# Second-layer matmuls moved inside an iteration, and the later keys projected from rounded halves

## The chip, the cores and the metric

The kernel runs on one core of a Trainium2 chip. The metric is the device time of one execution in microseconds, given as the median of several runs. A profile of one further execution is read beside it. TensorE multiplies matrices into eight PSUM banks, VectorE, ScalarE and GpSimd work on elements, and SyncE's queue (SP) issues all transfers.

## The reference

Eight batch elements, eight heads, 576 positions, head width 64, 128 random features. First a linear attention:

```python
def phi(x):                                   # x is q or k, scaled by 64 ** -0.25
    h = np.einsum('bhsd,md->bhsm', x, omega) - sum(x * x) / 2
    return np.exp(h - np.max(h, axis=-1, keepdims=True)) / np.sqrt(m)
q_p, k_p = phi(q_s), phi(k_s)
kv, z = np.einsum('bhsm,bhsd->bhmd', k_p, v), np.sum(k_p, axis=2)
x = np.einsum('bhsm,bhmd->bhsd', q_p, kv) / (q_p . z + 1e-6)      # heads side by side: 4608 x 512
```

Then a feed-forward block on the 4608 rows of 512: `xn` is the layer norm of `x` times a gain, and the result is `x + relu(xn @ w_ch1) @ w_ch2`, with 2048 hidden values. All is fp32. The term `sum(x * x) / 2` is the same for all features of a row and falls out when the maximum is subtracted.

## The kernel before

**Tiles.** The 4608 rows are nine tiles of 512. For each tile TensorE does the first layer (f runs over 16 groups of 128 hidden values), and the second layer, which adds the products of all 16 groups up in four PSUM banks. Both layers work on rounded halves: each operand is a high part plus a low part in the rounded fp32 form, and a product is three matmuls (high by high, low by high, high by low). A run of such a matmul reads its moving operand in an order spread in runs of eight.

**From the third tile on** the first layer is done by `seven`, which computes a 2 by 2 block product with seven block products in place of eight. An iteration (tile t, g of 4, h of 2) has the products B11, T2, T1, T3, B21, B22 and N4, each six matmuls of 128 x 256 in `product` (L1124). They go to two banks, `one` (x and y) and `two` (v and z). VectorE and ScalarE put the results together in a buffer `u`: `second` (ScalarE copy L1194, VectorE addition L1187, done key `u2`), `fourth` (two additions, key `c22`), `third` (one addition of 512, key `cc`), and `first` and `third` write the rectified halves `hid` (L1211, L1213). Each iteration makes two groups of hidden values. Their second-layer work, `mm2` (L1270), is 24 matmuls of 128 x 256 for each group, and stands in the iteration after: once inside `seven`, where it yields from `between()`, and once behind it. In a tile's first iteration both are empty, as the two groups left over are done ahead of it. `hid` has two buffers, and a buffer is freed when its 24 matmuls are issued.

**Attention** is worked off beside this, about a tile ahead. Keys come in chunks of 128 positions (36 in all, 18 of them of the batch elements from the fifth on). `gen_k` projects a chunk: raw keys of two heads lie on partitions 0 to 63 and 64 to 127, and 8 full fp32 products of 64 rows (L653) fill two banks with 8 heads x 128 features. Then per bank a maximum (L565) and four exponentials (L583) into a `kp` buffer, of which there are two; odd chunks wait with their pair for the sums with the values (L620). Queries of the first four blocks are projected likewise (L700); the later ones by `gen_q2` from halves: raw queries lie twice, on partitions 0 to 63 and 64 to 127; ScalarE rounds all (L726), VectorE subtracts the rounded from the raw on the lower half (L728), and two matmuls of 512 columns with `om_hi` and `om_lo` follow (L1043). The maximum over the features of queries is GpSimd's (L759). The numerators (L833) give x, its statistics (L868) and `xn`, which is transposed (L969, L974) and, for the tiles of `seven`, combined (L990) and halved (L1016).

**Order.** All engines' instructions are issued in an order that a planner, `Plan`, makes when the kernel is built, from a cost for each step (`act`, `dve`, `us`) and a rank for each part. A part that yields `"get"` waits for a buffer, one that yields `wait` for a key. TensorE's feed-forward work has the last rank, so that attention matmuls are put into the stream as soon as they are planned to be ready. Results and buffers bound how far ahead attention gets: nine x tiles, three `kv` buffers, 14 `wide` buffers, and two PSUM banks (`b_at`) for all attention work. Weights of the second layer that leave room for this work are brought back by transfers (L429), and so are prepared sums of the first layer's weights (L502).

Of the kernel before, what the change touches and what calls it, by code (L numbers as in the profile page):

```python
# [14 lines left out]
F32R = mybir.dt.float32r  # L15
# [7 lines left out]
P = 128  # L23
B, H, S, D = 8, 8, 576, 64
M = 128
# [43 lines left out]
class Plan:  # L69
# [74 lines left out]
    def free(self, *names):  # L144
        for n in names:
            assert n not in self.places, n
            self.places[n] = self.cur.seen()
            self.cur.holds -= n[0] == "b" and 0 < self.cur.holds
            self.wake(lambda w: w[0] == "get" and n in w[1])

    def done(self, key):
        self.made[key] = self.cur.seen()
        self.wake(lambda w: w == ("wait", key))
# [41 lines left out]


@with_exitstack
def favor_ffn(ctx, tc, kT, kTr, vF, vR, qT, qD, omT, gT, w1, w2, out):

# [19 lines left out]
    def f32(ap):  # L221
        return ap.bitcast(F32)
# [13 lines left out]
    def dma(n):  # L236
        return "run", {SP: n * 4e-6 / 0.36}
# [13 lines left out]
    def wait(*key):  # L251
        return "wait", key
# [4 lines left out]
    def tile_of(tag, shape, dtype=F32, pool=None):  # L257
        pool = pool or (wp if tag[1].isdigit() and tag[0] == "w" else small if tag[0:2] in ("kv", "mb", "st") or tag[0] == "v" else sb)
        return pool.tile(shape, dtype, tag=tag, name=tag, bufs=1)
# [28 lines left out]
    eps = const.tile([P, 1], F32, name="eps")  # L288
    nc.gpsimd.memset(eps, EPS)

    nc.gpsimd.partition_all_reduce(tile_of("st5", [P, 64])[:, 0:1], eps, P, bass_isa.ReduceOp.max)

    def gen_ident():
        for blk in range(T // QB):
# [14 lines left out]
    if TILED:  # L309
        om = const.tile([P, M], F32, name="om")  # L310
        om_hi = const.tile([P, M], F32R, name="om_hi")
        om_lo = const.tile([P, M], F32R, name="om_lo")
    else:
        om = const.tile([P, 2, M], F32, name="om")
        nc.vector.memset(om, 0.0)
# [196 lines left out]
    def gen_keys():  # L512
        for b in range(B):
            if b == 1:
                yield wait("w", 2, GATE_K)
            if b % 2 == 0:
                t_kv = yield "get", n_kv
                kvs[b] = t_kv, heads_of(t_kv)

            for c in range(NFULL + (b % 2 == 0)):  # L520
                plan.cur.rank = NS * (b * S // T) + RK + 2 * c
                if c == NFULL:
                    t_kv = yield "get", n_kv
                    kvs[b + 1] = t_kv, heads_of(t_kv)
                first = n_first if b == 0 else ()
                k_turn = () if first else ((yield "get", turn["k"]),)
                t_k = yield "get", first + n_big
                kraw = tile_of(t_k, [P, NP, P])
                t_v = yield "get", first + n_v
                v = heads_of(t_v)  # L530
                plan.add(plan.cur.rank, gen_k(b, c, kraw, v, (t_k, *k_turn), t_v, n_kp + first))
# [5 lines left out]
    def kv_last(b):  # L537
        return kv_key(b, NFULL if b % 2 == 0 else NFULL - 1)

    pairs, held = {}, {}  # L540

    def gen_k(b, c, kraw, v, early, t_v, n_kp):
        rank = plan.cur.rank
        yield dma(2 * P * NP * P)
        nc.sync.dma_start(kraw, kT[b, c] if c < NFULL else kTr[b // 2])
        nc.sync.dma_start(v, vF[b, c] if c < NFULL else vR[b // 2])
        if c:
            yield wait("k", b, c - 1)
# [9 lines left out]
        def values():  # L558
            yield us(DVE, 0.08)
            nc.vector.memset(v[:, :, D : D + 1], 1.0)  # L560
            done(("v", b, c))
# [71 lines left out]
        def keep(n, s, t_b, pv):  # L633
# [8 lines left out]
            free(t_b)  # L642
            done((*kv_key(n, c), s))

        plan.add(rank, values())
        if TILED:
            t_b = yield "get", at_now(), 2
            yield us(PE, 1.15 if mlp_on else 1.0)
            pk = [bank(x).rearrange("p (a b) -> p a b", b=M) for x in t_b]
            for p in range(NP):  # L650
                for h in range(2):
                    a = slice(h * D, (h + 1) * D)
                    nc.tensor.matmul(pk[h][:, p], kraw[a, p], om[a], start=True, stop=True)  # L653
            for s in range(2):
                plan.add(rank, side(s, t_b[s], pk[s]))
        else:
            for s in range(2):
                t_b = yield "get", at_now()
                yield us(PE, 0.87)
                pk = bank(t_b).rearrange("p (a b) -> p a b", b=M)  # L660
                for p in range(2):
                    nc.tensor.matmul(
                        pk[:, 2 * p : 2 * p + 2], kraw[:, 2 * s + p], om, start=True, stop=True
                    )
                plan.add(rank, side(s, t_b, pk))
# [74 lines left out]
    def gen_om2():  # L740
        yield dve(M)
        nc.vector.tensor_copy(om_hi, om)
        yield dve(M)
        nc.vector.tensor_tensor(out=om_lo, in0=om, in1=f32(om_hi), op=ALU.subtract)
        done(("om2",))

    def features(blk, j, s, t_b, pq):
# [38 lines left out]
    def gen_block(blk, b_turn):  # L786
        rank = plan.cur.rank
        for j in range(2):
            if blk < WHOLE:
                plan.add(rank, gen_q(blk, j))  # L790
            else:
                for s in range(2):
                    plan.add(rank, gen_q2(blk, j, s))
        t_st = yield "get", n_st
        st = tile_of(t_st, [P, 64])
        for i in range(2):
            plan.add(rank + 6 + 2 * i, gen_x(2 * blk + i, t_st, st))
        for j in range(2):
            for s in range(2):
                yield wait("phi", blk, j, s)  # L800
        yield wait("num", 2 * blk)
        yield wait("num", 2 * blk + 1)
        plan.add(rank + 8, gen_over(blk, t_st))
        free(*(phis[blk, j, s][0] for j in range(2) for s in range(2)), b_turn)
# [324 lines left out]
    def seven(t, g, h, between):  # L1129


        cs = slice(h * P, (h + 1) * P)
        if not both:
            both.extend((yield "get", b_h, 2))
            both.extend(bank(x) for x in both[:2])
            (t_u,) = yield "get", n_w[2, SHARED[3]], 1
            both.append(tile_of(t_u, [P, 4, HC]))
        one, two, u = both[2:]
        x, y, v, z = one[:, 0:HC], one[:, HC:], two[:, 0:HC], two[:, HC:]

        def plain(row, col):
            def left(k, l):
                if row == col == 0:
                    return wparts[1, NK * g][:, k, l, cs]
                return wparts[1, NK * g + 2 * col + k][:, row, l, cs]
            return left

        def ring(i):
            def left(k, l):
                return rings[t, g, i][1][:, l, k, cs]  # L1150
            return left

        def run(out, i, left, name, start=False):
            if i:
                yield wait("ring", t, g, i)
                left = ring(i)
            for j in range(2):
                yield wait("x2", t, name, j)
            yield us(PE, 6 * 0.1134)
            product(out, left, ops[t, name][1], start)  # L1160
            if i and h == 1:
                free(rings[t, g, i][0])
            if g == NK - 1 and h == 1:
                free(ops[t, name][0])

        before = (t, g, h - 1) if h else (t, g - 1, 1) if g else (t - 1, NK - 1, 1)
        before = before if before[0] >= SEVEN else None
        yield wait("moved", g)
        yield "get", ("one",)
        yield from run(x, 0, plain(0, 0), "B11", True)  # L1170
        yield from run(y, 2, None, "T2")
        plan.add(MOST_URGENT, second(t, g, h, before, x, y, u))
        yield "get", ("two",)
        yield from run(v, 1, None, "T1", True)
        yield from run(z, 3, None, "T3")
        plan.add(MOST_URGENT, fourth(t, g, h, before, v, z, u))
        yield wait("u2", t, g, h)
        yield from run(x, 0, plain(0, 1), "B21")
        plan.add(MOST_URGENT, first(t, g, h, x, u))
        yield from between()  # L1180
        yield wait("c22", t, g, h)
        yield from run(v, 4, None, "B22")
        yield from run(z, 0, plain(1, 1), "N4")
        plan.add(MOST_URGENT, third(t, g, h, before, two, u))
# [14 lines left out]
    def fourth(t, g, h, before, v, z, u):  # L1199
        if before:  # L1200
            yield wait("hid", before[0], NK * before[1] + 2 + before[2])
        yield wait("u2", t, g, h)
        yield dve(HC)
        add(u[:, 3], v, u[:, 0])
        yield dve(HC)
        add(u[:, 3], z, u[:, 3])
        done(("c22", t, g, h))
# [167 lines left out]
SHARED, HOSTS = (4, 5, 6, 7, 2, 3, 0, 1), 8  # L1375
LENT = (*SHARED, *(f + HOSTS for f in SHARED))
LEAVE, RSIDE = 24, 24
WARM, COLD = 0.0, 5.0
RW, RS = -10, 1.0
RK, RQ = -36, -28  # L1380
# [52 lines left out]
```

## Time and profile before

| | |
|---|---|
| median of 3 runs | 968.72 us (968.61 to 970.42) |
| the profiled execution | 969.5 us, of which the span is 967.7 us |
| busy in the span | TensorE 956.8, VectorE 655.2, ScalarE 414.7, GpSimd 141.6 us |
| granted TensorE clock | 1.00 on average |
| instructions | 22723 |

The span is the time from the first to the last instruction of the program that the profiler recorded; the execution's own time also holds what lies around it. A matmul's end is modelled and lies behind the next one's start, so a busy share says that TensorE was never without a matmul, not how many it could have done; distances between starts say that.

### The profile page before, as it was taken

Reading aid. Unit: us, or ns where it says so; the run is one execution under the profiler, and the core shown is the slowest. Engines: PE = TensorE matmul, PEld = TensorE weight load, DVE = VectorE, ACT = ScalarE, POOL = GpSimd, SP = SyncE. Lnnn points to the kernel's source line nnn. Section 1 sums busy time; section 2 is a strip of 40 time slices with the busy share of each in tenths; the row PEclk is TensorE's granted clock in tenths of the full one; section 3 lists DMA queues with packets and bytes.
Section 4 is the critical chain, followed back from the end, with each engine's and each line's share of the span. In section 5 each row is a group of like instructions: output and inputs, shape, how many; then the busy total and the mean of one; then the engine's idle time right before and its main releaser. Section 6 shows DMA issues by size and latency. Waiting matters only on the chain.

```text
span 967.7 us, 22723 instructions
## 1 busy us (share of the span) xinstructions
PE 956.8 (99%) x9302; PEld 885.6 (92%) x9302; DVE 655.2 (68%) x1455; ACT 414.7 (43%) x989; POOL 141.6 (15%) x80
## 2 busy tenths in 40 slices
PE   9999999999999999999999999999999999999998
PEld 7778778887889999999999999999999999999998
DVE  5999999768988855794569547684688367345333
ACT  6488755443554634462336324461544132122111
POOL 3201434000323300140012200330023000000000
PEclk9999999999999999999999999999999999999999
DMA  9179742556646676856775567565765575568641
GB/s 338 39 257 408 249 153 79 178 178 203 215 154 218 208 229 216 256 178 199 231 251 175 178 206 268 201 215 193 235 222 183 177 249 162 190 212 268 214 145 44
DMA packets 73031, 197.77 MB, mean 204 GB/s; under 512 B 7776, under 2 KB 16096, under 8 KB 72928
## 3 DMA queue, kind: packets, MB, share of 16 engines
q1 hardware_dynamic: 72928, 196.33, 61.4%
q8 instruction: 73, 1.20, 0.5%
q14 instruction: 30, 0.25, 0.1%
HBM read 170.08 MB, written 26.21 MB: 203 GB/s over the span
## 4 chain that ended last, share of the span: by engine, by line
PE 83%; DVE 11%; DMA 3%; issue 1%; SPq 0%; ACT 0%; POOL 0%; DVEq 0%; ACTq 0%; POOLq 0%
PE b L1270 31%; PE b L1124 27%; PE b L1043 14%; PE b L833 3%; PE b L653 3%; PE b L620 3%; DMA w<-w 2%; DVE wide L762 1%; PE b L969 1%; DVE wide L383 1%; DVE mb L565 1%; DVE w L369 1%; DVE w L990 1%; DMA w<-vF 1%; DVE w L402 1%
## 5 line engine op out<-in xcount | busy, mean ns | idle before, releaser
L1270 PE MATMUL b<-w,hid 128*128 128x256 f32 x2688 | 333.5, 277 | 0.0
L1270 PEld LDWEIGHTS b<-w,hid 128*128 128x128 f32 x2688 | 318.2, 188 | 4.3
L759 POOL PARTITION_ALL_REDUCE wide<-wide x72 | 140.5, 1975 | 602.5 <-ACT wide L241 274.1
L1124 PE MATMUL b<-xnT,w 128*128 128x256 f32 x1344 | 177.3, 278 | 2.5 <-DVE w L1187 2.3
L1124 PEld LDWEIGHTS b<-xnT,w 128*128 128x128 f32 x1344 | 163.9, 188 | 6.2 <-DVE w L1187 4.3
L1187 DVE TENSOR_TENSOR w<-b,w 128x256 f32<-128x256 f32 x224 | 109.4, 488 | 54.6 <-PE b L1124 39.5
L1124 PE MATMUL b<-w,w 128*128 128x256 f32 x1008 | 127.3, 277 | 0.0
L1124 PEld LDWEIGHTS b<-w,w 128*128 128x128 f32 x1008 | 120.0, 188 | 1.4
L1213 DVE SCALAR_TENSOR_TENSOR hid<-w,hid 128x256 fp32r<-128x256 f32 x112 | 63.3, 565 | 80.4 <-ACT hid L1211 79.5
L1211 ACT ACTIVATE hid<-w 128x256 fp32r<-128x256 f32 x112 | 58.0, 524 | 135.2 <-DVE w L1187 69.9
L1043 PE MATMUL b<-w,hid 128*128 128x512 f32 x384 | 96.6, 392 | 0.0
L1043 PE MATMUL b<-xnT,w 128*128 128x512 f32 x360 | 91.5, 393 | 0.0
L583 ACT ACTIVATE kp<-b,mb 128x128 f32<-128x128 f32 x256 | 70.7, 385 | 42.3 <-DVE mb L565 42.1
L1211 ACT ACTIVATE hid<-b 128x256 fp32r<-128x256 f32 x56 | 21.6, 386 | 154.7 <-PE b L1270 140.5
L1043 PEld LDWEIGHTS b<-w,hid 128*128 128x128 f32 x384 | 70.5, 188 | 14.2 <-DVE hid L1107 0.2
L1213 DVE SCALAR_TENSOR_TENSOR hid<-b,hid 128x256 fp32r<-128x256 f32 x56 | 23.7, 423 | 84.8 <-ACT hid L1211 84.5
L1043 PEld LDWEIGHTS b<-xnT,w 128*128 128x128 f32 x360 | 66.1, 188 | 14.9 <-issue 1.3
L565 DVE TENSOR_REDUCE mb<-b 128x4 f32<-128x512 f32 x72 | 46.6, 682 | 20.6 <-PE b L653 20.6
L241 ACT COPY wide<-b 128x512 f32<-128x512 f32 x70 | 40.2, 592 | 42.3 <-PE b L1043 30.2
L767 ACT ACTIVATE wide<-wide 128x512 f32<-128x512 f32 x72 | 45.7, 638 | 28.9 <-DVE wide L762 26.5
L762 DVE TENSOR_TENSOR wide<-wide,wide 128x512 f32<-128x512 f32 x64 | 49.4, 775 | 7.4 <-POOL wide L759 7.3
L728 DVE TENSOR_TENSOR wide<-wide,wide 64x512 fp32r<-64x512 f32 x56 | 42.8, 771 | 8.8 <-ACT wide L726 7.2
(98 smaller groups left out, 982.4 us busy)
## 6 DMA issues: line engine op xcount, KB each, us to landing
w<-side SPq DMA_DIRECT2D x112, 512.0 KB, 6.4
w<-kept SPq DMA_DIRECT2D x112, 512.0 KB, 4.1
w<-w SPq DMA_DIRECT2D x32, 512.0 KB, 7.7
wide<-qD SPq DMA_DIRECT2D x56, 256.0 KB, 4.3
out<-x SPq DMA_DIRECT2D x36, 256.0 KB, 3.7
kept<-w SPq DMA_DIRECT2D x16, 512.0 KB, 3.3
side<-wide SPq DMA_DIRECT2D x32, 256.0 KB, 2.9
v<-vF SPq DMA_DIRECT2D x28, 260.0 KB, 5.1
```

Of the source, the lines that this page charges most:

```text
L565: nc.vector.tensor_reduce(out=mb[:, 4 * s : 4 * s + 4], in_=pk, axis=AX.X, op=ALU.max, negate=True)
L583: nc.scalar.activation(out=kp[:, j], in_=pk[:, i], func=AF.Exp, scale=1.0, bias=mb[:, j : j + 1])
L728: nc.vector.tensor_tensor(out=qs[D:P], in0=qraw[D:P], in1=f32(qs[D:P]), op=ALU.subtract)
L759: nc.gpsimd.partition_all_reduce(mx, qc, P, bass_isa.ReduceOp.max)
L762: nc.vector.tensor_tensor(out=qc, in0=pq if direct else qc, in1=mx, op=ALU.subtract)
L767: nc.scalar.activation(out=qc, in_=qc, func=AF.Exp)
L1043: nc.tensor.matmul(out.rearrange("p (c a b) -> p c a b", a=AW, b=BW), lhsT, rhs.rearrange("p (a c b) -> p c a b", a=AW, b=BW), start=start ...
L1124: nc.tensor.matmul(passes(out), left(k, l), passes(right[:, r, k]), start=start and k + l + r == 0, stop=k + r == 2, skip_group_check=True,)
L1187: nc.vector.tensor_tensor(out=out, in0=left, in1=right, op=ALU.add)
L1211: nc.scalar.activation(out=hl[:, 0, cols], in_=x, func=AF.Relu)
L1213: nc.vector.scalar_tensor_tensor(out=hl[:, 1, cols], in0=x, scalar=0.0, in1=f32(hl[:, 0, cols]), op0=ALU.max, op1=ALU.subtract)
L1270: nc.tensor.matmul(accs[i].rearrange("p (c a b) -> p c a b", a=AW, b=BW)[:, :, n * 8 : n * 8 + 8], hl[:, l, cs], w[:, r, n * HC : (n + 1) ...
```

## The change

The first edit moves one line in `seven`: `yield from between()`, the 24 second-layer matmuls, comes behind T3 and ahead of the wait for `u2`, where it was behind B21.

The second edit projects the keys of the batch elements 4 to 7 (`ROUND = 4`) as the later queries already are. The host lays these keys out twice, on partitions 0 to 63 and 64 to 127, in two transfers of four heads each (`kD`, `kDr`). `halved_keys` rounds them on ScalarE and subtracts on VectorE; `joined` multiplies each head's 128 x 128 stationary block by `om_both`, which holds omega's high and low part side by side, 256 columns, two heads to a bank; `summed` copies the low part's product out of PSUM and adds the high part's to it; maximum and exponentials then run from SBUF. `om_both` is made once in `gen_om2`. The raw loads are no longer issued with the values' load but behind the taking of a `kp` buffer. The statistics buffers `st` shrink from 64 to 32 columns.

```diff
@@ favor_ffn
+        om_both = const.tile([P, 2 * M], F32R, name="om_both")
@@ gen_keys
+                if b >= ROUND:
+                    t_v = yield "get", n_v
+                    plan.add(plan.cur.rank, gen_k(b, c, None, heads_of(t_v), k_turn, t_v, n_kp))
+                    continue
                 t_k = yield "get", first + n_big
@@ gen_k
-        yield dma(2 * P * NP * P)
-        nc.sync.dma_start(kraw, kT[b, c] if c < NFULL else kTr[b // 2])
+        yield dma((2 if kraw is not None else 1) * P * NP * P)
+        if kraw is not None:
+            nc.sync.dma_start(kraw, kT[b, c] if c < NFULL else kTr[b // 2])
         nc.sync.dma_start(v, vF[b, c] if c < NFULL else vR[b // 2])
...
+        def halved_keys(s):
+            t_k = yield "get", n_big
+            raw = tile_of(t_k, [P, 4 * P])
+            yield dma(4 * P * P)
+            nc.sync.dma_start(raw, kD[b - ROUND, c, s] if c < NFULL else kDr[b // 2 - ROUND // 2, s])
+            t_s = yield "get", n_big
+            ks = tile_of(t_s, [P, 4, P], F32R)
+            flat = ks.rearrange("p a b -> p (a b)")
+            yield act(4 * P)
+            nc.scalar.copy(out=flat, in_=raw)
+            yield dve2(4 * P)
+            nc.vector.tensor_tensor(out=flat[D:P], in0=raw[D:P], in1=f32(flat[D:P]), op=ALU.subtract)
+            free(t_k)
+            splits[b, c, s] = t_s, ks
+            done(("ks", b, c, s))
+
+        def joined(s):
+            yield wait("ks", b, c, s)
+            t_s, ks = splits.pop((b, c, s))
+            t_b = yield "get", at_now(), 2
+            plan.cur.after = max(plan.cur.after, plan.cur.end + LATE)
+            yield us(PE, 4 * 0.1134)
+            pk = [bank(x).rearrange("p (i l m) -> p i l m", i=2, l=2) for x in t_b]
+            for i in range(4):
+                nc.tensor.matmul(
+                    pk[i // 2][:, i % 2].rearrange("p l m -> p (l m)").rearrange("p (c a b) -> p c a b", a=8, b=8),
+                    ks[:, i], om_both.rearrange("p (a c b) -> p c a b", c=4, b=8), start=i % 2 == 0, stop=True,
+                    skip_group_check=True,
+                )
+            free(t_s)
+            o = kp[:, 4 * s : 4 * s + 4]
+            for h in range(2):
+                plan.add(rank, summed(s, h, t_b[h], pk[h]))
+            for h in range(2):
+                yield wait("kh", b, c, s, h)
+            yield dve2(4 * M)
+            nc.vector.tensor_reduce(out=mb[:, 4 * s : 4 * s + 4], in_=o, axis=AX.X, op=ALU.max, negate=True)
+            for j in range(4 * s, 4 * s + 4):
+                yield act(M, 1, 0.175)
+                nc.scalar.activation(out=kp[:, j], in_=kp[:, j], func=AF.Exp, scale=1.0, bias=mb[:, j : j + 1])
+            done(("kp", b, c, s))
+
+        def summed(s, h, t_b, pk):
+            o = kp[:, 4 * s + 2 * h : 4 * s + 2 * h + 2]
+            yield act(2 * M, 1, 0.13)
+            nc.scalar.copy(out=o, in_=pk[:, :, 1])
+            yield dve(2 * M)
+            nc.vector.tensor_tensor(out=o, in0=pk[:, :, 0], in1=o, op=ALU.add)
+            free(t_b)
+            done(("kh", b, c, s, h))
+
         plan.add(rank, values())
-        if TILED:
+        if kraw is None:
+            yield wait("om2")
+            plan.add(rank, halved_keys(0))
+            plan.add(rank, halved_keys(1))
+            plan.add(rank, joined(0))
+            yield from joined(1)
+        elif TILED:
@@ gen_om2
+        pieces = om_both.rearrange("p (a l c b) -> p l c a b", l=2, c=2, b=8)
+        nc.scalar.copy(out=pieces[:, 0], in_=f32(om_hi).rearrange("p (c a b) -> p c a b", c=2, b=8))
+        yield us(ACT, 0.25)
+        nc.scalar.copy(out=pieces[:, 1], in_=f32(om_lo).rearrange("p (c a b) -> p c a b", c=2, b=8))
@@ gen_block
-        st = tile_of(t_st, [P, 64])
+        st = tile_of(t_st, [P, 32])
@@ seven
         yield from run(z, 3, None, "T3")
         plan.add(MOST_URGENT, fourth(t, g, h, before, v, z, u))
+        yield from between()
         yield wait("u2", t, g, h)
         yield from run(x, 0, plain(0, 1), "B21")
         plan.add(MOST_URGENT, first(t, g, h, x, u))
-        yield from between()
         yield wait("c22", t, g, h)
```

## Rows read from the trace of the kernel before

**Rows 1.** The page: busy time of each engine, and the granted clock by slices.

```profile
PE 956.8 (99%) x9302; PEld 885.6 (92%) x9302; DVE 655.2 (68%) x1455; ACT 414.7 (43%) x989; POOL 141.6 (15%) x80
...
PEclk9999999999999999999999999999999999999999
```

**Rows 2.** The list of waits of TensorE's matmuls: us, times, longest us.

```profile
PE b L1124 <- DVE w L1187: 2.3, 4, 1.2
```

**Rows 3.** The instructions of L653, 317 to 697 us.

```profile
L653 PE MATMUL b<-om,wide x288: 272/272/373, 317.0 to 695.8; 64*128 64x128 f32 x144
```

**Rows 4.** Busy time of each engine in three stretches.

```profile
core 0: us, PE busy (x) PEld busy (x) DVE busy (x) ACT busy (x) POOL busy (x), PEclk, DMA share, GB/s
...
80.00:120.00 40.00, 40.00 (x318) 31.41 (x317) 39.91 (x70) 32.53 (x70) 13.73 (x6) 1.00 0.86 321
...
317.00:697.00 380.00, 379.54 (x4029) 367.19 (x4029) 244.22 (x564) 162.88 (x421) 52.75 (x28) 1.00 0.66 216
...
436.00:480.00 44.00, 44.00 (x426) 43.87 (x425) 20.87 (x47) 13.93 (x34) 1.05 (x1) 1.00 0.64 204
```

**Rows 5.** Timeline of TensorE around a key chunk and query halves: start, us, what.

```profile
420.52 2.20 PE L1270 MATMUL b<-w,hid 128*128 128x256 f32 x18
422.65 1.16 PE L653 MATMUL b<-om,wide 64*128 64x128 f32 x16
423.74 0.99 PE L1270 MATMUL b<-w,hid 128*128 128x256 f32 x6
424.57 2.21 PE L1124 MATMUL b<-w,w 128*128 128x256 f32 x18
...
432.56 0.39 PE L1043 MATMUL b<-wide,om_hi 128*128 128x512 f32 x1
432.79 0.40 PE L1043 MATMUL b<-wide,om_lo 128*128 128x512 f32 x1
433.02 1.52 PE L1124 MATMUL b<-xnT,w 128*128 128x256 f32 x12
```

**Rows 6.** Timeline of the ninth tile's second iteration (g 0, h 1).

```profile
885.89 2.20 PE L1124 MATMUL b<-w,w 128*128 128x256 f32 x18
...
887.27 1.21 DVE L1213 SCALAR_TENSOR_TENSOR hid<-w,hid 128x256 fp32r<-128x256 f32 x2 [0.48 <-ACT hid L1211]
...
889.66 2.88 PE L1270 MATMUL b<-w,hid 128*128 128x256 f32 x24
...
892.38 1.52 PE L1124 MATMUL b<-xnT,w 128*128 128x256 f32 x12
```

**Rows 7.** Groups of instructions by shape, 317 to 697 us: busy, mean ns, idle before.

```profile
L1187 DVE TENSOR_TENSOR w<-b,w 128x256 f32<-128x256 f32 x87 | 36.6, 420 | 14.8 <-PE b L1124 9.0 <-ACT w L1194 4.8
...
L728 DVE TENSOR_TENSOR wide<-wide,wide 64x512 fp32r<-64x512 f32 x28 | 19.5, 708 | 5.0 <-ACT wide L726 4.2
...
L726 ACT CAST wide<-wide 128x512 fp32r<-128x512 f32 x28 | 17.0, 617 | 7.8 <-DMA wide<-qD 7.8
...
L1194 ACT COPY w<-b 128x256 f32<-128x256 f32 x28 | 10.5, 374 | 19.0 <-PE b L1124 18.4
L990 DVE TENSOR_TENSOR w<-w 128x256 f32<-128x256 f32 x13 | 9.9, 761 | 0.3 <-ACT w L974 0.2
```

**Rows 8.** The page's transfers by line: KB each, us to landing.

```profile
wide<-qD SPq DMA_DIRECT2D x56, 256.0 KB, 4.3
```

**Rows 9.** Timeline at four places: idle us in brackets (PEld is the weight load).

```profile
332.10 0.39 PE L1043 MATMUL b<-wide,om_lo 128*128 128x512 f32 x1
332.63 0.97 PE L1124 MATMUL b<-xnT,w 128*128 128x256 f32 x6
...
492.65 1.64 PE L1124 MATMUL b<-xnT,w 128*128 128x256 f32 x12 [0.30 <-DVE w L1187]
...
738.30 0.76 PEld L1124 LDWEIGHTS b<-xnT,w 128*128 128x128 f32 x6 [1.37 <-DVE w L1187]
...
888.87 0.76 PEld L1124 LDWEIGHTS b<-xnT,w 128*128 128x128 f32 x6 [0.29 <-DVE w L1187]
```

More of the change, by code (lines that the diff above doesn't have):

```diff
@@ L197, in favor_ffn @@
 @with_exitstack
-def favor_ffn(ctx, tc, kT, kTr, vF, vR, qT, qD, omT, gT, w1, w2, out):
+def favor_ffn(ctx, tc, kT, kTr, kD, kDr, vF, vR, qT, qD, omT, gT, w1, w2, out):
     nc = tc.nc
@@ L289, in favor_ffn @@
     nc.gpsimd.memset(eps, EPS)
-    nc.gpsimd.partition_all_reduce(tile_of("st5", [P, 64])[:, 0:1], eps, P, bass_isa.ReduceOp.max)
+    nc.gpsimd.partition_all_reduce(tile_of("st5", [P, 32])[:, 0:1], eps, P, bass_isa.ReduceOp.max)
     def gen_ident():
@@ L538, in kv_last @@
         return kv_key(b, NFULL if b % 2 == 0 else NFULL - 1)
-    pairs, held = {}, {}
+    pairs, held, splits = {}, {}, {}
     def gen_k(b, c, kraw, v, early, t_v, n_kp):
         rank = plan.cur.rank
-        yield dma(2 * P * NP * P)
-        nc.sync.dma_start(kraw, kT[b, c] if c < NFULL else kTr[b // 2])
+        yield dma((2 if kraw is not None else 1) * P * NP * P)
+        if kraw is not None:
+            nc.sync.dma_start(kraw, kT[b, c] if c < NFULL else kTr[b // 2])
         nc.sync.dma_start(v, vF[b, c] if c < NFULL else vR[b // 2])
@@ L744, in gen_om2 @@
         nc.vector.tensor_tensor(out=om_lo, in0=om, in1=f32(om_hi), op=ALU.subtract)
+        yield us(ACT, 0.25)
+        pieces = om_both.rearrange("p (a l c b) -> p l c a b", l=2, c=2, b=8)
+        nc.scalar.copy(out=pieces[:, 0], in_=f32(om_hi).rearrange("p (c a b) -> p c a b", c=2, b=8))
+        yield us(ACT, 0.25)
+        nc.scalar.copy(out=pieces[:, 1], in_=f32(om_lo).rearrange("p (c a b) -> p c a b", c=2, b=8))
         done(("om2",))
@@ L1377 @@
 LEAVE, RSIDE = 24, 24
+ROUND = 4
 WARM, COLD = 0.0, 5.0
@@ L1402 @@
     kTr = kTr.reshape(B // 2, P, NP, P)
+    k5 = k.reshape(B, NP, 2, S, D).transpose(0, 2, 4, 1, 3)[ROUND:]
+    k5 = np.concatenate([k5, k5], axis=2)
+    kD = np.ascontiguousarray(k5[..., : NFULL * P].reshape(B - ROUND, 2, P, 4, NFULL, P).transpose(0, 4, 1, 2, 3, 5))
+    kD = kD.reshape(B - ROUND, NFULL, 2, P, 4 * P)
+    kDr = k5[..., NFULL * P :].reshape((B - ROUND) // 2, 2, 2, P, 4, REM).transpose(0, 2, 3, 4, 1, 5)
+    kDr = np.ascontiguousarray(kDr).reshape((B - ROUND) // 2, 2, P, 4 * P)
     pad = np.zeros((B, S, H, D + 1), v.dtype)
@@ L1417 @@
     w2 = spread(moe_w_ch2.reshape(NF, P, DM)).view(np.int64)
-    arrays = {"kT": kT, "kTr": kTr, "vF": vF, "vR": vR, "qT": qT, "qD": qD, "omT": omT, "gT": gT, "w1": w1, "w2": w2}
+    arrays = {"kT": kT, "kTr": kTr, "kD": kD, "kDr": kDr, "vF": vF, "vR": vR, "qT": qT, "qD": qD, "omT": omT, "gT": gT, "w1": w1, "w2": w2}
     nc = bacc.Bacc("TRN2", target_bir_lowering=False, num_devices=1, dynamic_dma_scratch_size=64)
@@ L1427 @@
         with tc.manual_schedule():
-            favor_ffn(tc, *(aps[n] for n in ("kT", "kTr", "vF", "vR", "qT", "qD", "omT", "gT")), aps["w1"].bitcast(U32), aps["w2"].bitcast(U32), out)
+            favor_ffn(tc, *(aps[n] for n in ("kT", "kTr", "kD", "kDr", "vF", "vR", "qT", "qD", "omT", "gT")), aps["w1"].bitcast(U32), aps["w2"].bitcast(U32), out)
     if not nc.is_finalized():
```

## The prediction

> **What bounds the kernel now.** I read the page first: its first section says which engine is full, its second whether TensorE's clock is in question. TensorE is busy 99% of the span at the full granted clock, VectorE 68%, ScalarE 43% [rows 1]. Here "busy" overstates, because matmuls overlap in the records; what counts is the distance between their starts. So I took the list of what TensorE waited for, and then its timeline, matmul by matmul, from the start of the third tile on. The list has only 2.3 us of matmul waits on VectorE, in 4 waits, under the first layer's products (L1124) [rows 2]. What is left is a stream without gaps. A change here gains by taking matmul time out of that stream, and loses by making the stream wait; work for VectorE, ScalarE and the queues is free until TensorE waits for it.
>
> The stretches tell how much room there is. From 317 to 697 us, where all 18 key chunks of the batch elements from the fifth on are projected [rows 3], TensorE is busy 379.5 of 380 us, VectorE 244, ScalarE 163, the DMA engines 66% [rows 4]. Between 436 and 480 us GpSimd has 1.05 us of work, VectorE 20.9 of 44: the attention work has run as far ahead as its buffers let it (nine x tiles, freed by the results at a tile's end) and stands until the tile ends. That pause of some 44 us in a tile of about 97 us is the slack that the attention chain has.
>
> **Part one: keys from rounded halves.** Removed per chunk: the projection at L653, 8 products of 64 rows in full fp32, recorded as 16 matmuls. Their price in the stream is more than their own time. Take the chunk at 422.65 us [rows 5]: from 420.52 to 424.57 us the timeline has 18 second-layer matmuls, the projection, and 6 more. The undisturbed pace is 24 matmuls of 256 columns from 889.66 to 892.38 us [rows 6], 0.1133 us each, so these 24 take 2.72 us. 4.05 - 2.72 = 1.33 us is what one chunk costs: 1.09 us from its first start to the next matmul's, the rest lost around the border between the fp32 matmuls and the others (the 6 behind it take 0.83 us and not 0.68).
>
> Added per chunk: 8 matmuls of 128 rows against om_both, 256 columns each, in the same rounded form as the stream. No such key matmul is in the trace. The nearest rows are the query projections from halves at L1043, 512 columns each: two of them take from 432.56 to 433.02 us, 0.23 us each and so 0.115 per 256 columns, and the first-layer matmuls follow without a lost step [rows 5]; the other is the pace above, whose L1124 matmuls read in the same strided runs of eight. Both say 8 x 0.1133 = 0.91 us and no border. The lower bound is 0.91; the upper is what a chunk costs now, 1.33, as if each of its two groups of four lost 0.2 us. I take 0.91, since both nearest rows stand there. The gain is 1.33 - 0.91 = 0.42 us a chunk, 18 x 0.42 = 7.6 us; the bounds are 0 and 7.6.
>
> What is added elsewhere per chunk, from the same stretch [rows 7]: two casts of 512 on ScalarE as at L726 (0.617 each) and four PSUM copies of 256 as at L1194 (0.374): 2.73 us. On VectorE two half-height subtractions as at L728 (0.708) and four PSUM additions of 256 as at L1187 (0.420): 3.10 us. The maxima and exponentials stay in number and read SBUF where they read PSUM. Over 18 chunks ScalarE gets 49 us and VectorE 56 us: in the 380 us stretch 163 becomes 212 (56%) and 244 becomes 300 (79%). Costed at nothing: the cover is TensorE's stream, and from 80 to 120 us VectorE is busy 39.9 of 40 us while TensorE is busy all 40 [rows 4]. If that cover failed wholly, the 56 us would be the price; the bounds are 0 and 56. The two-instruction copy of omega into om_both happens once, on a ScalarE that is 43% busy: nothing.
>
> The load: 256 KB per chunk become 512 KB, in two transfers; 18 x 256 KB = 4.7 MB more over 380 us, 12 GB/s where 216 are moved [rows 4]. They are issued behind the halt for a key buffer, where the raw key load went ahead of it. A like transfer, queries for their halves, lands after 4.3 us [rows 8], to which come a cast and a subtraction, 1.3 us: a chunk's chain becomes some 6 us longer, with the later copy and addition 7 us. About four chunks belong to a tile, so at worst, all in series, 28 us a tile. The pause of 44 us covers it. On SP's queue the issues stand among those for the returning weights; they are in order, so a load may wait as those do, inside the same pause.
>
> PSUM: the pair of banks that a chunk held through four exponentials is now held for a copy and an addition, twice. It is handed back sooner, but asked for twice. Nothing either way.
>
> **Part two: the 24 matmuls moved.** In each (tile, g, h) from the third tile on the order was B11, T2, T1, T3, B21, 24 second-layer matmuls, B22, N4, 24. The wait in front of B21 is for `u2`, an addition behind T2. The change puts the 24 ahead of that wait, 2.72 us of cover. The timeline shows where the wait costs now: 1.37 us by the weight load's row at 738.30 us, 0.29 at 888.87, and from 332.10 (a query matmul of 0.23) to 332.63 us another 0.30 [rows 9]. Together 1.96; I take 2.0 us, all removed. The bounds are 1.66, the two waits that the rows name, and 2.3, all that the list has on VectorE [rows 2]. Not removed: the pause of 0.30 us in front of B22 at 492.65 us, in the fifth tile's first iteration, where no second-layer matmuls are left to stand between.
>
> What is late next: the moved 24 need the previous iteration's `hid`, now 0.68 us earlier. The tightest place is the ninth tile's second iteration: products start at 885.89 us, so T3 ends 24 x 0.1133 later, 888.61, and the first of two VectorE instructions that write `hid` from 887.27 ends near 887.7 [rows 6]. 0.9 us remain there. A late subtraction in front of it could use that up in up to 7 such iterations; at the 0.7 us of one subtraction that is near nothing. Of the first relu, the wait for a `hid` buffer was on these same 24 already, so x's bank is freed with 36 matmuls of cover, 4.1 us, as before. `c22` keeps its cover, 30 matmuls behind T3.
>
> **Sum.** The profiled execution took 969.5 us, its span being 967.7; the median of the runs is 968.72, 0.8 lower, and I state the forecast against the median. 968.72 - 7.6 - 2.0 = 959.1. I add 1.2 us for new waits: four like the one in front of B22, as VectorE goes from 64% to 79% of the stretch. Forecast 960.3 us.
>
> **The rivals.**
> A. *The gain is partly returned in waits.* VectorE's new instructions stand in front of `c22`, `u2` or `hid` additions. For it: attention work comes in bursts at a tile's start, and differences of transposed x written at L990 take 0.761 us where 256 columns cost 0.42 [rows 7], so something lengthens them at times; 36 new subtractions have the same shape of two SBUF inputs. The Trainium skill, SBUF — State Buffer, "Who interferes with whom", says that a VectorE instruction with two SBUF inputs contends with a GpSimd instruction that reads SBUF; the longer L990 agree, though no row names the cause. Against it: the saturated stretch without a wait. 13 to 25 waits of the 0.3 us seen in front of B22 on top of 959.1: 963 to 966.6 us.
> B. *The keys come late (slower).* A tile's first products stand until x is there. It begins when a tile's attention takes over 44 us longer, 11 us a chunk by four chunks. Beyond it four tiles wait: at 11.6 us a chunk the 2.4 us x 4 = 9.6 us eat the whole gain; at 13 us a chunk 4 x 8 = 32 us, near 992 us. Against it: my chain is 7 us a chunk and two chunks can overlap.
> C. *The projection gains nothing.* The groups of four stand apart and each loses its 0.2 us, at a wait for the late subtraction for example. Then only the move remains: 968.72 - 2.0 = 966.7, with a new wait or two 967 to 968.7. Against it: the 28 query pairs of the same build, cast, subtraction and matmul, lose nothing in the same stretch.
>
> **How the numbers follow.** Forecast (958 to 963): 0.72. A: 0.16. B: 0.07. C: 0.05. The range that leaves out no more than 2 in 10 has for its lower end no new wait (959.1), the B22 pause filled too (0.3), the wider bound of part two (0.3) and 0.7 us for waits under the list's threshold and the runs' spread: 957.8. Its upper end reaches through the better half of A, 965.0. About 0.2% (1.9 us) is what a measurement of this kernel can tell from no change: under 966.8 is faster. Forecast and A make that 0.88, C 0.05 for the same, B 0.07 for slower.
>
> **What would show it.** In the changed profile: 288 matmuls fewer at L653 and 144 new ones of 128 x 256; the next matmul of another line 0.11 us behind each group of four; no idle time in front of B21 in iterations other than a tile's first; VectorE near 711 us busy, ScalarE near 464; TensorE's waits on VectorE under 3 us. Wrong would be: key groups with 0.2 us lost around them (C), idle time of microseconds at a tile's first products (B), or many short waits on `u[...]` or `hid` between 317 and 697 us (A).

## The result, and the profile after

The changed kernel takes 962.06 us (median of 6 runs, 958.63 to 963.82) beside 970.25 us for the kernel before on the same chip (6 runs, 968.61 to 971.12). The ratio is 0.9911, 95% interval 0.9895 to 0.9927: 8.6 us faster, 7.1 to 10.2; the two medians lie 8.2 us apart. The forecast was 8.4 us, from 968.72 to 960.3. The profiled execution took 963.48 us, its span is 961.7. In two of the experiments below one execution took 2.4 or 3.3 ms; the ratios leave those two out.

The page of the changed kernel, its first two sections, answers to [rows 1]:

```profile
PE 950.6 (99%) x9158; PEld 882.1 (92%) x9158; DVE 704.4 (73%) x1578; ACT 451.6 (47%) x1084; POOL 140.9 (15%) x80
...
PEclk9999999999999999999999999999999999999999
```

TensorE has 144 matmuls fewer, VectorE 49 us more work and ScalarE 37 over the whole span (56 and 49 were worked out); TensorE's share and clock are as before. The new key matmuls, and TensorE's timeline around one group of four (start, us, what), answer to [rows 3, 5]:

```profile
L675 PE MATMUL b<-om_both,wide x144: 274/275/391, 313.6 to 695.9; 128*128 128x256 f32 x144
```

```profile
382.87 1.52 PE L1192 MATMUL b<-w,w 128*128 128x256 f32 x12
384.23 0.61 PE L675 MATMUL b<-om_both,wide 128*128 128x256 f32 x4
384.69 0.84 PE L1192 MATMUL b<-w,w 128*128 128x256 f32 x6
385.37 1.52 PE L1192 MATMUL b<-xnT,w 128*128 128x256 f32 x12
```

The four take from 384.23 to 384.69 us, 0.46, and the six behind them 0.68, the undisturbed pace. A chunk is two such groups, 0.92 us, and has no border. Before it was 1.33. This one place stands for the others: reckoned in the same way from the starts around each group, a chunk cost 1.35 us in all 18 places before, and 31 of the 36 new groups cost 0.454 us; the other five are longer, three of them by 0.5 to 0.7 us, with a wait beside them.

The stretches answer to [rows 4]:

```profile
core 0: us, PE busy (x) PEld busy (x) DVE busy (x) ACT busy (x) POOL busy (x), PEclk, DMA share, GB/s
...
317.00:697.00 380.00, 377.85 (x3929) 369.46 (x3930) 295.34 (x673) 206.39 (x525) 56.34 (x30) 1.00 0.69 231
436.00:480.00 44.00, 43.91 (x447) 43.13 (x446) 32.45 (x74) 22.64 (x58) 5.51 (x3) 1.00 0.64 207
```

VectorE has 295 us of work in the stretch of the keys (300 were worked out) and ScalarE 206 (212). In the pause from 436 to 480 us VectorE now has 32.5 us where it had 20.9: the attention work has spread into it, as it could.

The list of what TensorE waited for answers to [rows 2] (us in total, times, longest):

```profile
PE b L1096 <- DVE wide L985: 1.4, 1, 1.4
PE b L1111 <- DVE kp L698: 1.3, 3, 0.6
PE b L324 <- DVE spin L286: 1.2, 1, 1.2
PE b L1192 <- DVE w L1255: 1.1, 3, 0.4
PE b L1111 <- DVE wide L791: 0.8, 1, 0.8
```

The first and third lines were there before (1.4 and 1.2 us) and lie ahead of the third tile. The waits of first-layer products on additions fell from 2.3 to 1.1 us: none is left in front of B21, and three stand in front of B22 in first iterations of tiles, at 491, 697 and 880 us, where before had two. And 2.1 us of new ones stand at L1111, at query projections, three behind VectorE's key additions and one behind the subtraction for the query itself. From the third tile on the list thus went from 2.3 to 3.2 us. The ninth tile's second iteration answers to [rows 6], and to the last of [rows 9]:

```profile
880.99 2.20 PE L1192 MATMUL b<-w,w 128*128 128x256 f32 x18
...
882.37 1.21 DVE L1281 SCALAR_TENSOR_TENSOR hid<-w,hid 128x256 fp32r<-128x256 f32 x2 [0.48 <-ACT hid L1279]
...
883.71 2.88 PE L1338 MATMUL b<-w,hid 128*128 128x256 f32 x24
...
886.43 1.75 PE L1192 MATMUL b<-xnT,w 128*128 128x256 f32 x14
```

The 24 matmuls follow T3 without idle time at the place where `hid` was tightest, and B21 follows them without any.

**Where the 8.6 us show in the traces.** The third tile's first product starts at 278.22 us before and at 280.31 after. The windows view gives the stretch up to there, first of the kernel before, then of the changed one:

```profile
0.00:278.22 278.22, 274.36 (x2326) 220.02 (x2327) 239.36 (x500) 162.78 (x364) 66.21 (x40) 1.00 0.60 206
```

```profile
0.00:280.31 280.31, 276.21 (x2326) 220.17 (x2327) 242.12 (x508) 160.09 (x359) 64.22 (x40) 1.00 0.59 204
```

The same 2326 matmuls took 2.1 us longer. From there to the end of the span before took 967.7 - 278.2 = 689.5 us and after 961.7 - 280.3 = 681.4: 8.1 us less. So the profiled span is 6.0 us shorter; the medians differ by 8.2, as the execution profiled before lay 0.75 us under its kernel's median and the one after 1.4 us over its own. Not all of the 8.1 us is TensorE's. The last results are put together here, first before, then after:

```profile
961.26 2.79 DVE L1286 SCALAR_TENSOR_TENSOR x<-b,rss,x 128x512 f32<-128x512 f32 x4 [1.99 <-PE b L1270]
```

```profile
955.99 2.79 DVE L1354 SCALAR_TENSOR_TENSOR x<-b,rss,x 128x512 f32<-128x512 f32 x4 [1.99 <-PE b L1338]
```

From the third tile's first product to there it is 7.4 us less (683.0 and 675.7). The other 0.7 us lie behind, while the last results leave (6.4 and 5.7 us), and were not explained.

### The profile page after: what moved, and what is told of

Its sections match the earlier page's. It is cut to its first block, busy times and chain, and to the rows that moved or that the text cites. A ratio compares the mean times of both kernels' runs of the same rounds, so it can differ in the third digit from the quotient of the medians.

```text
span 961.7 us, 22725 instructions
## 1 busy us (share of the span) xinstructions
PE 950.6 (99%) x9158; PEld 882.1 (92%) x9158; DVE 704.4 (73%) x1578; ACT 451.6 (47%) x1084; POOL 140.9 (15%) x80
## 4 chain that ended last, share of the span: by engine, by line
PE 85%; DVE 8%; DMA 5%; ACT 1%; issue 1%; SPq 0%; DVEq 0%; ACTq 0%
PE b L1338 28%; PE b L1192 25%; PE b L1111 21%; PE b L626 3%; PE b L901 3%; DMA wide<-qD 2%; PE b L716 1%; PE b L675 1%; DVE w L1058 1%; DMA wide<-kD 1%; DVE w L1255 1%; PE b L1037 1%; DMA w<-w 1%; DVE wide L830 1%; DMA w<-vF 1%
## 5 line engine op out<-in xcount | busy, mean ns | idle before, releaser
L1192 PE MATMUL b<-xnT,w 128*128 128x256 f32 x1344 | 175.1, 277 | 1.1 <-DVE w L1255 1.1
L1111 PE MATMUL b<-w,hid 128*128 128x512 f32 x384 | 97.1, 395 | 0.0
L1111 PE MATMUL b<-xnT,w 128*128 128x512 f32 x360 | 92.8, 397 | 0.2 <-ACT xnT L1100 0.2
L1111 PEld LDWEIGHTS b<-w,hid 128*128 128x128 f32 x384 | 70.8, 188 | 15.9 <-issue 0.3
L1111 PEld LDWEIGHTS b<-xnT,w 128*128 128x128 f32 x360 | 66.0, 188 | 16.0 <-issue 1.0
L690 ACT ACTIVATE kp<-kp,mb 128x128 f32<-128x128 f32 x144 | 51.6, 397 | 11.3 <-DVE mb L687 10.7
L789 ACT CAST wide<-wide 128x512 fp32r<-128x512 f32 x56 | 34.4, 619 | 25.7 <-DMA wide<-qD 20.8
```

Source lines behind the costliest of these rows:

```text
L690: nc.scalar.activation(out=kp[:, j], in_=kp[:, j], func=AF.Exp, scale=1.0, bias=mb[:, j : j + 1])
L1111: nc.tensor.matmul(out.rearrange("p (c a b) -> p c a b", a=AW, b=BW), lhsT, rhs.rearrange("p (a c b) -> p c a b", a=AW, b=BW), start=start ...
L1192: nc.tensor.matmul(passes(out), left(k, l), passes(right[:, r, k]), start=start and k + l + r == 0, stop=k + r == 2, skip_group_check=True,)
```

## The experiments

Each was timed beside the kernel before; ratios are to that. "Changed kernel" is the one with both edits.

**The two edits alone.** First the move, with the keys as before:

```diff
+        yield from between()
         yield wait("u2", t, g, h)
         yield from run(x, 0, plain(0, 1), "B21")
         plan.add(MOST_URGENT, first(t, g, h, x, u))
-        yield from between()
```

> Only the 24 second-layer matmuls are moved ahead of the wait for u2; the keys are projected as before. My theory (the gain is TensorE time of the key projections, 7.6 us, and u2 waits, 2.0 us): 1 to 2.5 us faster than before, with no idle time in front of B21 where the 24 matmuls stand. Rival (the move is most of the gain, since it changes the planner's whole order): 5 us or more faster.

Measured: 968.53 us, ratio 0.9978 (0.9966 to 0.9990), 2.1 us faster. The two waits of the first-layer products that its profile still lists, 0.8 us, stand in first iterations of tiles, the third and the ninth, where there are no 24 matmuls to move. The move alone is worth what was worked out for it. But it also brings a wait of a kind that the changed kernel has, with no new work on VectorE:

```profile
435.74 0.46 PE L1043 MATMUL b<-wide,om_hi 128*128 128x512 f32 x1 [0.96 <-DVE wide L728]
```

A new order of the instructions is enough for a query projection to wait.

Then the keys, with the 24 matmuls behind B21 (the same diff turned round, in the changed kernel):

> Only the keys from the fifth batch element on are projected from rounded halves; the 24 matmuls stay behind B21. My theory: 7.6 us of TensorE time less 1 to 3 us of new waits, so 5 to 7 us faster than before. Rival (the projection gains nothing, the move does): within 2 us of before.

Measured: 968.26 us, ratio 0.9965 (0.9951 to 0.9980), 3.4 us faster (1.9 to 4.8), less than the theory's 5 to 7 us; the rival's 2 lies at the edge of the interval. Its waits and two of its places show a part of why:

```profile
PE b L1192 <- DVE w L1255: 3.8, 8, 0.7
```

```profile
612.54 1.52 PE L1192 MATMUL b<-w,w 128*128 128x256 f32 x12
613.90 0.84 PE L1192 MATMUL b<-xnT,w 128*128 128x256 f32 x6
615.45 0.96 PE L1192 MATMUL b<-xnT,w 128*128 128x256 f32 x6 [0.71 <-DVE w L1255]
...
746.77 0.46 PE L1111 MATMUL b<-wide,om_hi 128*128 128x512 f32 x1 [1.35 <-DVE x L916]
```

Eight waits of first-layer products, 3.8 us, stand where before had four and 2.3 us, and the changed kernel three and 1.1 us. Three of the eight, 1.5 us, are B21's wait for `u2`, which the 24 matmuls would cover. One is shown: T3 begins at 613.90 us, its six take 0.68, and B21 starts at 615.45, 0.87 us late. The other five, 2.3 us, stand in front of B22 in first iterations of tiles, where the move changes nothing, and a query projection waits 1.4 us.

Singly the edits bring 2.1 + 3.4 = 5.5 us, together 8.6. The difference of 3.1 us has an interval of some 2.4 us to either side (an estimate from the three intervals). The move does cover work that the other edit gives to VectorE, but by the trace that is the smaller part of the 3.1: by starts, the waits in front of B21 outside first iterations cost some 2.9 us here and 2.0 before. Why the other waits are fewer with both edits was not tried.

**The border between fp32 and rounded matmuls.** The kernel before, each later projection in two halves:

```diff
-            yield us(PE, 1.15 if mlp_on else 1.0)
+            yield us(PE, (0.6 if b >= 4 else 1.15) if mlp_on else 1.0)
...
             for p in range(NP):
+                if b >= 4 and p == 2:
+                    plan.cur.after = plan.cur.end + 0.3
+                    yield us(PE, 0.6)
                 for h in range(2):
```

> The kernel before, but each of the 18 later key projections is cut into two groups of 4 fp32 products with a few rounded matmuls between them; the work is the same. My theory (0.24 us or more of a chunk's 1.33 us is lost at the border between fp32 and rounded matmuls): one more border a chunk, 18 x 0.24 to 0.33 = 4 to 6 us slower than before. Rival (the projection costs its own columns only, the border nothing): within 1 us of before.

Measured: 977.37 us, ratio 1.0067 (1.0049 to 1.0086), 6.5 us slower for 18 borders more, 0.36 us each (0.26 to 0.46). The timeline of one chunk:

```profile
592.36 2.88 PE L1273 MATMUL b<-w,hid 128*128 128x256 f32 x24
595.17 0.72 PE L656 MATMUL b<-om,wide 64*128 64x128 f32 x8
595.82 0.99 PE L1273 MATMUL b<-w,hid 128*128 128x256 f32 x6
596.74 0.71 PE L656 MATMUL b<-om,wide 64*128 64x128 f32 x8
597.38 3.80 PE L1273 MATMUL b<-w,hid 128*128 128x256 f32 x31
```

The six matmuls between the groups take 0.92 us and not 0.68, and the two groups 0.65 and 0.64 us where the undivided one took 1.09. From the starts around it a chunk costs 1.75 us in all 18 places, where it cost 1.35: 0.40 us for a border, 7.2 us in all, which fits the 6.5. So 0.36 to 0.40 us of a chunk's 1.35 were the border, and some 0.95 to 0.99 the products themselves. Of the gain of some 0.44 us a chunk all but 0.04 to 0.08 is the border that is gone. The old projection differs from the stream around it in its number form and in its 64 rows; which of the two makes the border was not separated.

**Is VectorE's work covered?** The changed kernel with the maxima taken twice:

```diff
             nc.vector.tensor_reduce(out=mb[:, 4 * s : 4 * s + 4], in_=o, axis=AX.X, op=ALU.max, negate=True)
+            yield dve2(4 * M)
+            nc.vector.tensor_reduce(out=mb[:, 4 * s : 4 * s + 4], in_=o, axis=AX.X, op=ALU.max, negate=True)
```

> The changed kernel with every maximum of the later keys taken twice on VectorE, the same result; 36 more instructions of 0.68 us, 24.5 us more VectorE work. My theory (VectorE work is covered by TensorE's stream): at most 2 us slower than the changed kernel. Rival A (VectorE is near its limit in the stretch, and what it gets comes back as waits): 6 us or more slower than the changed kernel, most of the gain gone.

Measured: 962.07 us, ratio 0.9901 (0.9884 to 0.9918), not slower than the changed kernel. Its page has VectorE at 723.4 us where the changed kernel has 704.4: 19 us more, where 24.5 were expected. That much more work costs nothing, so VectorE's sum isn't what returns part of the gain.

**The raw loads behind the key buffer.** The changed kernel with both loads issued beside the values' load:

```diff
+                    t_ks = yield "get", n_big, 2
...
+            for s in range(2):
+                raws.append(tile_of(t_ks[s], [P, 4 * P]))
+                nc.sync.dma_start(raws[s], kD[b - ROUND, c, s] if c < NFULL else kDr[b // 2 - ROUND // 2, s])
...
-            t_k = yield "get", n_big
...
-            nc.sync.dma_start(raw, kD[b - ROUND, c, s] if c < NFULL else kDr[b // 2 - ROUND // 2, s])
```

> The changed kernel with the raw loads of the later keys issued beside the values' load, ahead of the taking of a key buffer, as before the change; two wide buffers a chunk are held for longer. My theory (the longer chain of a chunk lies in the attention work's pause and costs nothing): within 1 us of the changed kernel. Rival B (late keys set where key and query matmuls wait): 2 us or more faster.

Measured: 962.85 us, ratio 0.9917 (0.9902 to 0.9932), as the changed kernel. The load in a chunk's longer chain costs nothing where it now stands; the cast, the subtraction and the addition stay in the chain here, so their share is not tested.

**The waits that are left.** Two tries to remove them from the changed kernel. First no flush of the previous tile's two groups ahead of a first iteration:

```diff
-                if f == 0:
+                if f == 0 and t <= SEVEN:
                     yield from one()
                     yield from one()
```

> The changed kernel, but from the fourth tile on the two groups left over from the tile before are no longer done ahead of the first iteration; they stand inside it, as in every other iteration, so that no iteration is without its 24 matmuls in front of B21. My theory (the waits of 0.46 to 0.57 us at a tile's first iteration are all that is left of the u2 and c22 waits): these vanish, 1 to 3 us faster than the changed kernel. Rival (the waits there were filled by attention work anyway, and results leave a tile later): within 1 us of the changed kernel, or slower.

Measured: 963.28 us, ratio 0.9908 (0.9887 to 0.9928), no difference. The waits at first iterations are gone from its list, but two of 1.5 us stand at query projections, at 509 and 611 us, and the theory of 1 to 3 us fell. Then `LATE = 2.0`:

> The changed kernel with the planner's delay between VectorE's last step and the matmuls that use it doubled (LATE 2 for 1 us). My theory (2 to 3 us of the gain came back as waits of key, query and transpose matmuls that the planner put too early): these waits fall below 1 us in sum, 1 to 2 us faster than the changed kernel. Rival (the waits come from VectorE being late as a whole): they stay.

Measured: 964.73 us, ratio 0.9928 (0.9914 to 0.9942), no faster. The waits of query projections are gone from the third tile on, as meant, and yet the time did not fall: its list has one wait of 1.7 us at L1111 in the first two tiles, at 163 us, and 2.6 us in 6 waits of first-layer products, all in front of B22 in first iterations. The theory fell here too: with each new order of the instructions a few waits of 0.2 to 1.7 us stand somewhere else.

**More keys from halves.** The changed kernel with `ROUND = 2`:

> The changed kernel with the keys of the third and fourth batch elements, 9 chunks more, projected from halves as well, in the stage of the first two tiles. My theory (0.42 us or more of TensorE time a chunk): 9 x 0.42 = 3.8 us faster than the changed kernel, less new waits, so 1 to 4 us. Rival (VectorE is too full in that stage): no faster, or slower by 1 us and more.

Measured: 981.36 us, ratio 1.0103 (1.0089 to 1.0118), 10 us slower than before, where 1 to 4 us faster than the changed kernel were expected. The third tile's start, in this kernel:

```profile
280.00:310.00 30.00, 20.32 (x137) 17.36 (x138) 27.06 (x70) 16.81 (x43) 5.67 (x4) 0.72 0.53 172
```

TensorE has work for 20.3 of 30 us and its granted clock has a mean of 0.72: it goes down from its level of 2.4 GHz to that of 1.2 from 282.6 to 299.6 us, after the engine had stood without a matmul for 2.94 us up to 281.92. (A shorter fall, of 6.8 us, lies at 163 us.) VectorE is busy 27 of 30, so I put it down to VectorE, and left the fourth batch element's keys, which fall there, in fp32 (`if b == 2 or b >= 4`), without early loads and with them:

> The changed kernel with the keys of the third batch element, 5 chunks at 165 to 205 us, projected from halves too; those of the fourth, which fell into the start of the third tile where VectorE was the bound, stay in fp32. My theory (the loss with both was VectorE work at the third tile's start, where weights are summed and the first operands made): 5 x 0.42 = 2.1 us less TensorE time, 0 to 3 us faster than the changed kernel. Rival (any more halves on VectorE in the first two tiles' stage cost more than they bring): 2 us or more slower.

> The two edits of the runs beside it together: early raw loads, and the third batch element's keys from halves too. My theory: like the run with the third element's keys alone, within 1 us. Rival B: 2 us faster than that one.

Measured: 978.79 us (ratio 1.0084, 1.0069 to 1.0099) and 983.68 us (1.0145, 1.0125 to 1.0165). The theory fell. The windows and waits of the kernel with the third element's keys and late loads:

```profile
200.00:260.00 60.00, 60.00 (x434) 48.97 (x433) 42.20 (x90) 27.57 (x75) 0.00 (x0) 1.00 0.51 165
280.00:300.00 20.00, 12.84 (x74) 11.07 (x73) 17.23 (x43) 15.09 (x43) 5.28 (x4) 0.66 0.55 183
```

```profile
PE b L1037 <- ACT kp L589: 5.1, 1, 5.1
```

For 60 us up to 260 GpSimd, and so the queries' features, has nothing, while VectorE isn't full. The kernel before has 8.05 us of GpSimd's work in the same stretch, all of it from 240 us on, and so begins some 20 us earlier. Here the attention work for the third tile comes late, TensorE waits 5.1 us at a transpose until key exponentials (L589) are done, and VectorE has 17 of 20 us. This is what rival B describes: attention late at a tile's start. Earlier raw loads did not help but made it worse, so their latency is not the cause. What held the attention between 200 and 260 us (a buffer, the pair of PSUM banks, a rank) was not tried and stays open.

**The 2.1 us ahead of the third tile.** The kernel before with om_both's two copies in `gen_om2` and the smaller `st`, om_both not being used; then with om_both only set aside:

> The kernel before with om_both made by its two ScalarE copies and the smaller st, and nothing else: om_both is not used. In the changed kernel's profile the third tile starts 2.1 us later than in that of before, after the same matmuls, as more of the 512-column matmuls go at 230 ns and fewer at 220. My theory (the two copies change the order of the attention work from about 110 us on, and where the stream is interrupted decides at which of the two paces it goes on): the third tile starts near 280.3 us as in the changed kernel, and the whole is 1 to 3 us slower than before. Rival (chance of a run): third tile near 278.2 us and no difference.

> The kernel before with om_both only set aside in memory, not written, and the smaller st: the instructions and their order are those of before, only addresses move. The run with the two copies had its third tile at 280.5 us, before has it at 278.2. My theory (the order of the work decides at which pace the 512-column matmuls go on): third tile near 278.2 us, within 0.1% of before. Rival (addresses decide): third tile near 280.5 us, about 1 to 2 us slower than before.

Measured: 972.06 us, ratio 1.0010 (1.0001 to 1.0019), and 971.40 us, ratio 1.0001 (0.9989 to 1.0013). Their third tiles start at

```profile
280.50 2.20 PE L1130 MATMUL b<-w,w 128*128 128x256 f32 x18
```

```profile
278.21 2.20 PE L1125 MATMUL b<-w,w 128*128 128x256 f32 x18
```

So the addresses make no difference that shows. The two copies, which the prediction cost at nothing, change the planner's order, in TensorE's stream from about 115 us on, and the third tile starts 2.3 us later with it. Executions differ too: four of the kernels here, the one before among them, share one order of TensorE ahead of the third tile, and start it at 278.0 to 279.0 us; six, the changed one among them, share the other, and start it at 279.8 to 281.3. The ranges do not meet. In the median of all runs the copies cost about 1 us (0.1 to 1.8).

## Why the prediction was right

The main mechanism was right, the price of the key projection. The measured 962.06 us lies in the stated range (957.8 to 965.0), 1.8 us above the forecast time, and the kernel before took 1.5 us more on this chip than in the forecast. The closeness of 8.4 to 8.6 is in part luck, as other terms missed in both directions.

**The key projection** (7.6 us of TensorE time, 0.91 us a chunk, no border) was right by its own rows: 0.46 us for four, and 18 x (1.33 - 0.92) = 7.4 us; by the starts around all groups it is 7.9. That the price before was in part a border, which the prediction read from the six slower matmuls, was shown by adding 18 borders: 0.36 us each. The border is nearly all of the gain.

**The move** (2.0 us, the `u2` waits) was right: 2.1 us alone (1.0 to 3.3). Its upper bound was misread: of the four waits in the list of 2.3 us three stand in first iterations, and only the one at 738.30 us is where the 24 matmuls come. The two edits were added up as independent; the runs say that they aren't. Without the move the keys bring 3.4 us and not 7.6. In the sum this made no difference, since both edits are there.

**New waits** were put at 1.2 us, like the one in front of B22, and this term was too small: the list has 2.1 at query projections and some 0.5 more in front of B22. By starts, counting each step that is over 0.12 us longer than the usual one between the same two kinds, TensorE lost some 3.7 us from the third tile on before (without the borders) and 4.7 after; -2.0 + 1.2 had been forecast. The sign "waits on VectorE under 3 us" was just missed, at 3.2. Rival A thus came in a weak form, and, by these runs, more from the order of the instructions than from VectorE's sum: the move alone has such a wait, and 19 us more VectorE work cost nothing in the changed kernel, which rules out the strong form. What was read right is that `hid` and x's bank keep their cover.

**Costed at nothing and not nothing**: the two copies for om_both. The planner's order moved, and the first two tiles' matmuls lost 2.1 us in the profile. From the third tile on the forecast was 9.6 - 1.2 = 8.4 us less; TensorE's stream shows 7.4, and 0.7 more lie behind its last matmul, in a place that the prediction had no term for. The profiled pair is 6.0 us apart and the medians 8.2, so a part of the agreement lies in which executions were profiled.

**Rival B** (late keys) did not come; that the pause of a tile covered the longer chain fits this, and early loads changed nothing. What B describes did come in the three kernels that take more keys from halves in the first two tiles. **Rival C** fell with the groups of four, which lose nothing around them.

What made some subtractions long, which the prediction left open, stands in the traces. The Trainium skill, SBUF — State Buffer, "Who interferes with whom", says that a VectorE instruction with two SBUF inputs contends with a GpSimd instruction that reads SBUF. The traces agree. Of the 36 new subtractions 27 run with no GpSimd instruction beside them and take 0.68 to 0.69 us; of the other nine, four take as long and five 1.19 to 1.53. The differences at L990 before are alike: 0.39 to 0.43 us without GpSimd, up to 1.26 with it. For the new subtractions this is 3.5 us of VectorE's work in all; that it cost TensorE anything is not shown.

## What to carry to other kernels

Price a matmul by the stretch of the stream that it displaces, from an undisturbed start to the next undisturbed start: here over a quarter of a projection's price was the border, much of it in its neighbours. When one edit loads an engine and another gives its results more time, time each alone before adding them up. A free share of an engine does not say that it can take more work: here it could where attention was a tile ahead, and more keys from halves cost time where it was not. Look at each stage's start. And a change of two small instructions can move the whole order that a planner makes; read the stretches that were not meant to change as well.

## What the hardware did that was not expected

The 512-column matmuls of the first two tiles go at one of two paces. TensorE's timeline of the kernel before and of the changed one, each over a stretch of one kind:

```profile
268.12 1.48 PE L1043 MATMUL b<-xnT,w 128*128 128x512 f32 x6
269.44 0.38 PE L1043 MATMUL b<-wide,om_hi 128*128 128x512 f32 x1
```

```profile
262.07 2.24 PE L1111 MATMUL b<-xnT,w 128*128 128x512 f32 x9
264.14 0.39 PE L1111 MATMUL b<-wide,om_hi 128*128 128x512 f32 x1
```

Six take 1.32 us, 0.220 each; nine take 2.07 us, 0.230 each, at the same granted clock. The same kinds of matmul go at either pace, and the kernel with the two copies alone has the slower pace in this place and the kernel with moved addresses the faster one, so the order in which other work interrupts the stream has to do with it. It is not the order alone: of some 735 steps from one 512-column matmul to the next ahead of the third tile, 295 to 370 take under 0.225 us in the four kernels with the order of before, and 145 to 273 in the six with that of the changed one. What in TensorE holds a pace was not found.
